# More chunks of the down product in three reduced-precision parts, with the high parts of activations taken by VectorE and ScalarE in turns

## The chip, the cores and the metric

The kernel runs on one core of a Trainium2 chip. The metric is the device time of one execution in microseconds; the kernel before takes 281.24 us (median of three runs, 281.20 to 281.31). One further execution was taken with the profiler, and all durations below come from it.

## What is computed

An attention block with polynomial sketches is followed by a feed-forward block (SwiGLU). Cut to what matters:

```python
# attention: q, k, v are (4, 4, 1088, 32); S1, S2 are (8, 32)
phi(x) = outer(S1 @ x, S2 @ x)             # 64 features per position
kv, z  = sum_s phi(k) v, sum_s phi(k)      # per batch and head
attn   = (phi(q) @ kv) / (phi(q) @ z + 1e-6)
# feed-forward over 4352 tokens of width 128, hidden width 1536
g   = x @ w_gate
out = (g * sigmoid(g) * (x @ w_val)) @ w_out
```

All inputs and outputs are float32.

## The kernel before

Everything is kept transposed: tokens lie along the free dimension, features on partitions. Tokens are cut into blocks: three small ones of batch 0 (384, 384 and 320 tokens), then seven "line" blocks that cover batches 1 to 3, six of 480 tokens and a last one of 384. The line blocks are numbered 0 to 6 here. The hidden width of 1536 is cut into 12 chunks of 128.

The line blocks are worked in one software pipeline over y = 0 to 83 (`END`, the loop at L1355): turn y belongs to block y // 12 and chunk y % 12, which together are one unit. A turn issues, in this order:

- `start_unit(y + 1)`: two matmuls on the "difference" parts of weights and tokens (L977) into a pair of PSUM banks, then ScalarE scales both banks in place (L980).
- `finish_unit(y)`: first the work that earlier turns put down in the table `before` for this turn; then four matmuls that add to the pair (L990, L991); Silu on ScalarE (L993); the gated product on VectorE (L998), which makes the hidden chunk and gives the pair of banks free; then the work that was put down in the table `behind`.
- `down`: the down product of a unit that was finished about five turns earlier.
- `parts_of`: a piece of the attention of batches 2 and 3; in turns 4, 6, 20, 22 and 40 a group of attention matmuls on PE stands ahead of the turn. `token_steps` cut the tokens of the next block into parts in listed turns.

There are three pairs of banks, handed out in turns by `pair`, so the pair of unit y is wanted again by the start of unit y + 3. In turns 20 and 40 (`WIDE`) the finish stands ahead of the next start. The lists fix the order on each engine; there is no planner at run time, and each engine takes its instructions in the order in which they were issued.

The matmuls of gate and value use three products of reduced precision (type fp32r) in place of one of full precision: a number a is cut into a high part a1 = a(1 - 2^-13) rounded to fp32r, a rest a0, and a difference made of both, and the product is put together from difference x difference, high x high and rest x rest. The down product can be done in the same way, and before the change it is for five chunks, (1, 4, 6, 8, 10), of each of blocks 3, 4 and 5 (`FINE`, `DOWN`, L895, L896):

- The parts of the weights are made by `cut_down` (L909), a generator that is taken one step further in each of the turns 24, 26, ... 36 (L1371): ScalarE makes the high part `w1`, GpSimd the rest `low`, ScalarE the scaled rest `wb`, GpSimd the difference `wd`. The other chunks of such a block use weights scaled by -4096 (`scaled`), so that they add to the differences in one bank.
- The parts of a hidden chunk are made by `cut_hidden` (L942): in turn y + 1 ScalarE makes the high part h1 (L954), in turn y + 2 GpSimd the rest h0 (L955), in turn y + 3 VectorE the difference hd (L958). Three sets of buffers serve in turns; they take the place of tiles that the attention no longer needs.
- `down` (L1041) then issues three matmuls (L1054 into one bank, L1056 and L1057 into a second) where it issues one of full precision otherwise (L1062). After chunk 10, `copy_out` has ScalarE copy the second bank (L1077), and after chunk 11 `put_together` has VectorE add the first (L1083); the store follows.

Block 2, and blocks 0, 1 and 6, are done with full-precision down products throughout.

Of the kernel before, what the change touches and what calls it, by code (L numbers as in the profile page):

```python
# [7 lines left out]
FP32 = mybir.dt.float32  # L8
F32R = mybir.dt.float32r
# [3 lines left out]
AF = mybir.ActivationFunctionType  # L13
ALU = mybir.AluOpType
# [5 lines left out]
def kernel(  # L20
# [28 lines left out]
    nc = tc.nc  # L49
    P = nc.NUM_PARTITIONS  # L50
    B, H, S, Dh = q.shape
    R = S1.shape[0]
    D, Dff = moe_w_gate.shape
# [5 lines left out]
    NCH = Dff // P  # L59
# [11 lines left out]
    WB = 480  # L71
# [9 lines left out]
    const = ctx.enter_context(tc.tile_pool(name="const", bufs=1))  # L81
    stage = ctx.enter_context(tc.tile_pool(name="stage", bufs=2))
    apool = ctx.enter_context(tc.tile_pool(name="attn", bufs=1))
# [29 lines left out]
    def bank(tag=None):  # L113

        if tag is not None:
            i = place[tag]
        elif oldest[0]:
            i = min((i for i in used if i not in held), key=used.get)
        else:
            i = place[free_banks[turn[0] % len(free_banks)]]  # L120
            turn[0] += 1
        touch(i)
        return PS[:, i, :]
# [31 lines left out]
    wo = const.tile([P, NCH, D], FP32, name="wo")  # L155
# [32 lines left out]
    def load_next():  # L188
# [36 lines left out]
        out=ident[:], in_=ident[:], pattern=[[-1, P]], base=0, channel_multiplier=1,  # L225
# [90 lines left out]
    late = const.tile([P, NL, BW], FP32, tag="late", name="late", bufs=1)  # L316
# [500 lines left out]
    BETA = 4096.0  # L817
    CUT = 1.0 - 2.0**-13
# [3 lines left out]
    def whole(ap):  # L822
        return ap.bitcast(FP32)
# [17 lines left out]
    def cut_weights(w, lows, engine):  # L841

        rows = [], [], [], []
        sub = dict(op=ALU.subtract)
        for c, (w1, wb, wd) in enumerate(homes(w)):
            src = w[:, 3 * c : 3 * c + 3, :]
            low = lows[c]
            w_parts[id(w), c] = (w1, wb, wd)
            fine = dict(out=wd, in0=whole(w1), in1=whole(wb), **sub), engine.tensor_tensor
            if engine is nc.vector:  # L850
                fine = dict(
                    out=wd, in0=low, scalar=-BETA, in1=whole(w1), op0=ALU.mult, op1=ALU.add
                ), engine.scalar_tensor_tensor
            for row, f, args in zip(
                rows,
                (nc.scalar.activation, engine.tensor_tensor, nc.scalar.activation, fine[1]),
                (
                    dict(out=w1, in_=src, func=AF.Copy, scale=CUT),
                    dict(out=low, in0=src, in1=whole(w1), **sub),
                    dict(out=wb, in_=low, func=AF.Copy, scale=BETA),  # L860
                    fine[0],
                ),
            ):
                row.append((f, args))
        return rows
# [26 lines left out]


    line = list(range(HEAD, len(blocks)))
    FINE, PLAIN = (1, 4, 6, 8, 10), (0, 2, 3, 5, 7, 9, 11)  # L895
    DOWN = [(i, j) for i in line[3:6] for j in FINE]  # L896
    down_parts = {}
    h_parts = {}
    h_sets = []
    before, behind = {}, {}  # L900

    def add_to(where, y, f):
        where.setdefault(y, []).append(f)

    def now(where, y):
        for f in where.pop(y, ()):
            f()

    def cut_down():  # L909

        n = len(FINE)
        parts = const.tile([P, 3, n, D], F32R, tag="late", name="dparts", bufs=1)
        w1, wb, wd = (parts[:, k] for k in range(3))
        scaled = apool.tile([P, len(PLAIN), D], FP32, tag="zs", name="scaled")
        low = [
            apool.tile([P, c, D], FP32, tag=tag, name="low" + tag)[:]
            for tag, c in (("kas", 2), ("kab2", 3))
        ]
        down_parts.update(w1=w1, wb=wb, wd=wd, scaled=scaled)
        cs = slice(0, 2), slice(2, 5)  # L920
        runs = [(0, slice(1, 5, 3)), (2, slice(6, 11, 2))]
        for k, c in runs:
            nc.scalar.activation(w1[:, cs[k > 0]], wo[:, c, :], AF.Copy, scale=CUT)
        yield
        for (k, c), x in zip(runs, low):
            nc.gpsimd.tensor_tensor(
                out=x, in0=wo[:, c, :], in1=whole(w1[:, cs[k > 0]]), op=ALU.subtract
            )
            yield
        for c, x in zip(cs, low):  # L930
            nc.scalar.activation(wb[:, c], x, AF.Copy, scale=BETA)
        yield
        for c in cs:
            nc.gpsimd.tensor_tensor(
                out=wd[:, c], in0=whole(w1[:, c]), in1=whole(wb[:, c]), op=ALU.subtract
            )
            yield
        for k, c in ((0, slice(0, 1)), (1, slice(2, 4)), (3, slice(5, 12, 2))):
            m = len(range(12)[c])
            nc.scalar.activation(scaled[:, k : k + m, :], wo[:, c, :], AF.Copy, scale=-BETA)  # L940

    def cut_hidden(y, i, j):  # L942

        if not h_sets:
            x = []
            for tag in ("kld", "qld", "vld", "kT", "qT"):
                t = const.tile([P, 2, WB], F32R, tag=tag, name="h" + tag, bufs=1)
                x += [t[:, k, :] for k in range(2)]
            h_sets.extend(x[k : k + 3] for k in range(0, 9, 3))
        n = blocks[i][1]  # L950
        h_sets.append(h_sets.pop(0))
        h1, h0, hd = h_parts[i, j] = [x[:, 0:n] for x in h_sets[-1]]
        h = hidden[i, j][:, 0:n]
        add_to(behind, y + 1, lambda: nc.scalar.activation(h1, h, AF.Copy, scale=CUT))  # L954
        add_to(before, y + 2, lambda: nc.gpsimd.tensor_tensor(  # L955
            out=h0, in0=h, in1=whole(h1), op=ALU.subtract
        ))
        add_to(before, y + 3, lambda: nc.vector.scalar_tensor_tensor(  # L958
            out=hd, in0=whole(h0), scalar=-BETA, in1=whole(h1), op0=ALU.mult, op1=ALU.add
        ))  # L960


    room = const.tile([P, 10, BW], FP32, tag="room", name="room", bufs=1)
# [18 lines left out]
    def finish_unit(y):  # L982
        i, j = line[y // NCH], y % NCH
        n = blocks[i][1]
        x1, x0, _ = (x[:, 0:n] for x in x_parts[i])
        ps = sums_of.pop(y)
        now(before, y)
        for k, w in enumerate((wg, wv)):
            w1, wb = (w_parts[id(w), j // 3][t][:, j % 3, :] for t in range(2))
            nc.tensor.matmul(ps[:, k], w1, x1, start=False, stop=False, skip_group_check=True)  # L990
            nc.tensor.matmul(ps[:, k], wb, x0, start=False, stop=True, skip_group_check=True)  # L991
        sg = fpool.tile([P, WB], FP32, tag="sg", name="sg", bufs=5)[:, 0:n]
        nc.scalar.activation(sg, ps[:, 0], AF.Silu, scale=WHOLE)  # L993
        slot_of[i, j] = slots.pop(0)
        hj = slot_of[i, j]
        hidden[i, j] = hj
        todo.append((i, j))
        nc.vector.scalar_tensor_tensor(  # L998
            out=hj[:, 0:n], in0=ps[:, 1], scalar=WHOLE, in1=sg, op0=ALU.mult, op1=ALU.mult
        )  # L1000
        let_go(y)
        now(behind, y)
        if (i, j) in DOWN:
            cut_hidden(y, i, j)
# [36 lines left out]
    def down(y=None):  # L1041
# [3 lines left out]
        if j == 0:  # L1045
            acc[i] = bank("g1" if i == 1 else "g2" if i in line[2::2] else "acc")
        mine = [c for c in range(NCH) if (i, c) in DOWN]
        if mine and j == mine[0]:
# [88 lines left out]
    for h in range(H):  # L1137
# [13 lines left out]
        out=s12[:],  # L1151
        in0=sTv.unsqueeze(1).to_broadcast([P, H, 2, R]),
        in1=own[:].unsqueeze(2).unsqueeze(3).to_broadcast([P, H, 2, R]),
        op=ALU.mult,
# [19 lines left out]
    n = steps[0][1]  # L1174
# [58 lines left out]
    def group():  # L1233
        while ahead[0] != "pe":
            ahead[0] = next(att)
        ahead[0] = next(att, "end")
# [34 lines left out]
    parts = {}  # L1271
# [8 lines left out]
    for z, (i, j) in enumerate(seq):  # L1280
# [16 lines left out]
        if z == 20:  # L1297
# [4 lines left out]
            first, low, second, third = cut_weights(wv, lows, nc.gpsimd)  # L1302
# [48 lines left out]
    oldest[0] = True  # L1351
    hold("acc")
    down_steps = cut_down()
    start_unit(0)
    for y in range(END):  # L1355
        if y in GROUPS:
            group()
        if y in WIDE:
            finish_unit(y)
        if y + 1 < END:  # L1360
            start_unit(y + 1)
        if y not in WIDE:
            finish_unit(y)
        for _ in range(2):

            if len(todo) > min(5 + (todo[0] == (line[1], 0)), END - y + 1):
                down(y)
        parts_of(y < EASY or y % 2 == 0)
        for gen in token_steps.get(y, ()):
            next(gen, None)  # L1370
        if y in range(24, 38, 2):  # L1371
            next(down_steps, None)
    ps = wide("a")[:, 0, 0:D]
    for j in range(NCH):
# [6 lines left out]
    b, x0 = divmod(t0 // 32, NX)  # L1381
# [34 lines left out]
```

## Time and profile before

| | before |
|---|---|
| median of three runs | 281.24 us |
| the profiled execution, whole | 281.56 us |
| its span, first to last instruction | 279.9 us |
| PE (matmul) busy | 273.3 us |
| PEld (weight loads) busy | 195.5 us |
| ScalarE (ACT) busy | 181.5 us |
| VectorE (DVE) busy | 174.3 us |
| GpSimd (POOL) busy | 76.9 us |
| mean granted TensorE clock | 1.000 |
| full-precision matmul records of L1062 on 480 tokens, mean | 565 ns (two records for each matmul) |
| a matmul of parts on 480 tokens, L1054 to L1057, mean | 377 to 382 ns |
| VectorE gated product L998, 480 tokens, mean | 657 ns |
| ScalarE high part L954, mean | 606 ns |
| GpSimd rest L955, mean | 1223 ns |
| VectorE difference L958, mean | 649 ns |

Busy times are the sums of the records' durations. Matmuls are pipelined, so that records overlap and their mean is longer than the spacing of one to the next; the chain of work that ended last shows the spacing. A group's row names the line, engine, operation, output tile and input tiles, shape, count, and then busy time, mean of one, and idle time ahead of it with what ended it. Idle time of an engine that isn't the bound costs nothing by itself.

### The profile page before, as it was taken

The page shows a single profiled execution, that of the slowest core. Times are in us where ns is not written, and L with a number is a line of the kernel's source. Part 1 is how long each engine was busy: PE and PEld are TensorE (multiplying, and loading weights), DVE is VectorE, ACT ScalarE, POOL GpSimd, SP SyncE. Part 2 cuts the span into 40 slices and gives each one's busy share as a digit, 9 for nine tenths or more (in the row PEclk, how much of TensorE's full clock was granted, in tenths as well). Part 3 has the DMA queues.
Part 4 walks back from the last instruction along what each step waited for, and adds up shares of the span by engine and source line. Part 5 has one row for each costly group of instructions (what it writes and reads, how often), then busy time and mean ns, then how long its engine had stood idle before and what let it go on. Part 6 is the DMA issues. An engine that isn't in the chain of part 4 may idle for free.

```text
span 279.9 us, 5561 instructions
## 1 busy us (share of the span) xinstructions
PE 273.3 (98%) x2154; PEld 195.5 (70%) x2154; DVE 174.3 (62%) x327; ACT 181.5 (65%) x323; POOL 76.9 (27%) x93
## 2 busy tenths in 40 slices
PE   7899999999999999999999999999999999999995
PEld 6645565666756687777577767757777778778994
DVE  3997987976688863887544565545436444644431
ACT  3468566555511686677457786869788888877860
POOL 3314422179720530160010140013313333131000
PEclk9999999999999999999999999999999999999999
DMA  6573195222041123000200020002000200100011
GB/s 193 164 226 78 49 284 171 82 80 80 20 108 28 27 85 91 2 1 2 36 13 4 0 39 0 0 2 35 1 0 2 35 0 0 23 15 1 9 30 28
DMA packets 26139, 14.30 MB, mean 51 GB/s; under 512 B 19840, under 2 KB 24192, under 8 KB 26112
## 3 DMA queue, kind: packets, MB, share of 16 engines
q1 hardware_dynamic: 25456, 13.84, 19.2%
q8 instruction: 17, 0.28, 0.4%
q10 hardware_dynamic: 656, 0.10, 0.2%
q14 instruction: 10, 0.08, 0.1%
HBM read 11.41 MB, written 2.23 MB: 49 GB/s over the span
## 4 chain that ended last, share of the span: by engine, by line
PE 94%; DVE 2%; DMA 2%; ACT 1%; issue 0%; SPq 0%
PE PS L1062 26%; PE PS L1014 16%; PE PS L990 13%; PE PS L977 13%; PE PS L991 13%; PE PS L783 2%; PE PS L357 2%; PE PS L345 2%; PE PS L391 2%; DMA kld<-in_k_dram 2%; PE PS L1057 1%; PE PS L1054 1%; PE PS L1056 1%; PE PS L1090 1%; PE PS L500 1%; PE PS L448 1%
## 5 line engine op out<-in xcount | busy, mean ns | idle before, releaser
L980 ACT ACTIVATE PS<-PS 128x960 f32<-128x960 f32 (+1 forms) x84 | 78.3, 934 | 37.1 <-PE PS L977 36.6
L998 DVE SCALAR_TENSOR_TENSOR hbuf<-PS,sg 128x480 f32<-128x480 f32 (+1 forms) x84 | 54.0, 643 | 75.2 <-ACT sg L993 74.9
L1062 PE MATMUL PS<-hbuf,wo 128*128 128x480 f32 (+3 forms) x142 | 57.5, 505 | 0.0
L977 PE MATMUL PS<-xd,gphq 128*128 128x480 f32 (+1 forms) x84 | 52.2, 622 | 0.0
L993 ACT ACTIVATE sg<-PS 128x480 f32<-128x480 f32 (+1 forms) x84 | 46.6, 555 | 2.0 <-PE PS L991 1.3
L990 PE MATMUL PS<-x,graw 128*128 128x480 f32 (+1 forms) x84 | 32.1, 382 | 0.6 <-ACT PS L980 0.6
L1062 PEld LDWEIGHTS PS<-hbuf,wo 128*128 128x128 f32 x142 | 26.6, 189 | 8.2 <-issue 0.9
L991 PE MATMUL PS<-x,wb 128*128 128x480 f32 (+1 forms) x84 | 31.6, 376 | 0.0
L977 PE MATMUL PS<-xd,wd 128*128 128x480 f32 (+1 forms) x84 | 31.4, 374 | 0.0
L990 PE MATMUL PS<-x,w 128*128 128x480 f32 (+1 forms) x84 | 31.4, 374 | 0.0
L991 PE MATMUL PS<-x,graw 128*128 128x480 f32 (+1 forms) x84 | 31.3, 372 | 0.0
L1014 PE MATMUL PS<-xT,wg 128*128 128x384 f32 (+1 forms) x72 | 28.7, 480 | 0.0
L1014 PE MATMUL PS<-xT,wv 128*128 128x384 f32 (+1 forms) x72 | 28.0, 470 | 0.2 <-DVE wv L289 0.2
L1018 ACT ACTIVATE sg<-PS 128x384 f32<-128x384 f32 (+1 forms) x30 | 13.9, 466 | 18.7 <-PE PS L1014 17.0
L977 PEld LDWEIGHTS PS<-xd,gphq 128*128 128x128 f32 x84 | 15.8, 188 | 12.5 <-ACT PS L980 9.6
L977 PEld LDWEIGHTS PS<-xd,wd 128*128 128x128 f32 x84 | 15.9, 189 | 12.2 <-issue 9.0
L1062 PE MATMUL PS<-hbuf,scaled 128*128 128x480 f32 x42 | 20.3, 564 | 0.0
L1014 PEld LDWEIGHTS PS<-xT,wv 128*128 128x128 f32 x72 | 13.4, 190 | 8.9 <-DVE hbuf L1029 0.9
L1014 PEld LDWEIGHTS PS<-xT,wg 128*128 128x128 f32 x72 | 12.9, 189 | 9.3 <-issue 1.2
L883 POOL TENSOR_TENSOR x<-xT,x 128x480 fp32r<-128x480 f32 (+1 forms) x6 | 7.1, 1178 | 42.8 <-ACT x L882 42.8
L990 PEld LDWEIGHTS PS<-x,graw 128*128 128x128 f32 x84 | 15.7, 187 | 4.3 <-ACT PS L980 1.6
L990 PEld LDWEIGHTS PS<-x,w 128*128 128x128 f32 x84 | 15.8, 188 | 2.1
(169 smaller groups left out, 409.8 us busy)
## 6 DMA issues: line engine op xcount, KB each, us to landing
kld<-in_k_dram SPq DMA_DIRECT2D x4, 544.0 KB, 4.4
vld<-in_v_dram SPq DMA_DIRECT2D x12, 144.0 KB, 4.6
qld<-in_q_dram SPq DMA_DIRECT2D x3, 544.0 KB, 3.5
raw<-in_moe_w_out_dram SPq DMA_DIRECT2D x4, 384.0 KB, 4.0
raw<-in_moe_w_gate_dram SPq DMA_DIRECT2D x3, 384.0 KB, 3.7
raw<-in_moe_w_val_dram SPq DMA_DIRECT2D x3, 384.0 KB, 3.6
out_dram<-o SPq DMA_DIRECT2D x16, 60.0 KB, 1.9
vld<-in_v_dram SPq DMA_DIRECT2D x4, 112.0 KB, 4.4
```

Of the source, the lines that this page charges most:

```text
L345: nc.tensor.matmul(ps[32 * a : 32 * a + 32, 96 * (c - c0) : 96 * (c - c0) + 96], qT[:, 4 * c + a, :], s123[:, a : a + H, :, :].rearrange(" ...
L357: nc.tensor.matmul(ps[32 * a : 32 * a + 64, 64 * (c - c0) : 64 * (c - c0) + 64], kT[:, c, a : a + 2, :].rearrange("p a t -> p (a t)"), s12 ...
L883: engine.tensor_tensor(out=x0[:, 0:n], in0=x, in1=whole(x1[:, 0:n]), op=ALU.subtract)
L977: nc.tensor.matmul(ps[:, k], w_parts[id(w), j // 3][2][:, j % 3, :], xd, start=True, stop=True)
L980: nc.scalar.activation(ps, ps, AF.Copy, scale=-1.0 / BETA / WHOLE)
L990: nc.tensor.matmul(ps[:, k], w1, x1, start=False, stop=False, skip_group_check=True)
L991: nc.tensor.matmul(ps[:, k], wb, x0, start=False, stop=True, skip_group_check=True)
L993: nc.scalar.activation(sg, ps[:, 0], AF.Silu, scale=WHOLE)
L998: nc.vector.scalar_tensor_tensor(out=hj[:, 0:n], in0=ps[:, 1], scalar=WHOLE, in1=sg, op0=ALU.mult, op1=ALU.mult)
L1014: nc.tensor.matmul(o[:, 0:n], w[:, j, :], xT[:, t0 : t0 + n], start=True, stop=True)
L1018: nc.scalar.activation(sg[:, 0:n], g[:, 0:n], AF.Silu)
L1062: nc.tensor.matmul(acc[i][:, 0:n], w, hidden[i, j][:, 0:n], **sides)
```

## The change

1. More chunks in parts: in blocks 3 to 5 the chunks 1, 2, 4, 5, 7, 8, 9 and 10 (eight in place of five), and in block 2, which had none, the chunks 2, 4, 6, 8, 9 and 10.
2. The high part of a hidden chunk is made by VectorE for the chunks 2, 5, 8 and 10 of blocks 3 to 5, in the table `before` of turn y + 1; for the others, and all of block 2, by ScalarE as before.
3. The weights' parts are made for ten chunks (1 to 10) and in turns 20 to 28, each step taking pieces of three, three and four chunks; the parts lie in the tile `room`, the rests in the place of the tile `late`.
4. There are six sets of buffers for the parts of hidden chunks; the new ones lie in the place of `late` too, after the rests.

```diff
-    FINE, PLAIN = (1, 4, 6, 8, 10), (0, 2, 3, 5, 7, 9, 11)
-    DOWN = [(i, j) for i in line[3:6] for j in FINE]
+    FINE, PLAIN = range(1, NCH - 1), (0, 1, 3, 5, 7, 6, NCH - 1)
+    DOWN = [(line[2], j) for j in (2, 4, 6, 8, 9, 10)]
+    DOWN += [(i, j) for i in line[3:6] for j in (1, 2, 4, 5, 7, 8, 9, 10)]
...
     def cut_down():
...
-        parts = const.tile([P, 3, n, D], F32R, tag="late", name="dparts", bufs=1)
+        parts = const.tile([P, 3, n, D], F32R, tag="room", name="dparts", bufs=1)
...
+        low = const.tile([P, n, D], FP32, tag="late", name="dlow", bufs=1)
...
+        def high(c):
+            nc.scalar.activation(w1[:, c], wo[:, FINE[0] :][:, c], AF.Copy, scale=CUT)
+        def left(c):
+            nc.gpsimd.tensor_tensor(
+                out=low[:, c], in0=wo[:, FINE[0] :][:, c], in1=whole(w1[:, c]), op=ALU.subtract
+            )
+        def scale(c):
+            nc.scalar.activation(wb[:, c], low[:, c], AF.Copy, scale=BETA)
+        def differ(c):
+            nc.gpsimd.tensor_tensor(
+                out=wd[:, c], in0=whole(w1[:, c]), in1=whole(wb[:, c]), op=ALU.subtract
+            )
+        def other(k, c):
+            m = len(range(NCH)[c])
+            nc.scalar.activation(scaled[:, k : k + m, :], wo[:, c, :], AF.Copy, scale=-BETA)
+        a, b, c = slice(0, 3), slice(3, 6), slice(6, n)
+        for step in (
+            [(high, a)], [(left, a), (high, b)], [(left, b), (scale, a)], [(differ, a), (high, c)],
+            [(left, c), (scale, b)], [(differ, b), (scale, c)], [(differ, c), (other, *rest[0])],
+            [(other, *rest[1])], [(other, *rest[2]), (other, *rest[3])],
+        ):
+            for f, *args in step:
+                f(*args)
             yield
...
     def cut_hidden(y, i, j):
...
-            h_sets.extend(x[k : k + 3] for k in range(0, 9, 3))
+            t = const.tile([P, 8, WB], F32R, tag="late", name="hlate", bufs=1)
+            x += [t[:, k, :] for k in range(8)]
+            h_sets.extend(x[k : k + 3] for k in range(0, 18, 3))
...
-        add_to(behind, y + 1, lambda: nc.scalar.activation(h1, h, AF.Copy, scale=CUT))
+        if j in (2, 5, 8, 10) and i != line[2]:
+            add_to(before, y + 1, lambda: nc.vector.tensor_scalar(h1, h, CUT, None, op0=ALU.mult))
+        else:
+            add_to(behind, y + 1, lambda: nc.scalar.activation(h1, h, AF.Copy, scale=CUT))
...
-        if y in range(24, 38, 2):
+        if y in range(20, 30):
             next(down_steps, None)
```

More of the change, by code (lines that the diff above doesn't have):

```diff
@@ L911, in cut_down @@
         n = len(FINE)
-        parts = const.tile([P, 3, n, D], F32R, tag="late", name="dparts", bufs=1)
+        parts = const.tile([P, 3, n, D], F32R, tag="room", name="dparts", bufs=1)
         w1, wb, wd = (parts[:, k] for k in range(3))
         scaled = apool.tile([P, len(PLAIN), D], FP32, tag="zs", name="scaled")
[L915 to L918, printed above, removed]
+        low = const.tile([P, n, D], FP32, tag="late", name="dlow", bufs=1)
         down_parts.update(w1=w1, wb=wb, wd=wd, scaled=scaled)
[L920 to L925, printed above, removed]
+        rest = [(0, slice(0, 1)), (1, slice(1, 8, 2)), (5, slice(6, 7)), (6, slice(NCH - 1, NCH))]
+        def high(c):
+            nc.scalar.activation(w1[:, c], wo[:, FINE[0] :][:, c], AF.Copy, scale=CUT)
+        def left(c):
             nc.gpsimd.tensor_tensor(
-                out=x, in0=wo[:, c, :], in1=whole(w1[:, cs[k > 0]]), op=ALU.subtract
+                out=low[:, c], in0=wo[:, FINE[0] :][:, c], in1=whole(w1[:, c]), op=ALU.subtract
             )
[L929 to L933, printed above, removed]
+        def scale(c):
+            nc.scalar.activation(wb[:, c], low[:, c], AF.Copy, scale=BETA)
+        def differ(c):
             nc.gpsimd.tensor_tensor(
@@ L936, in cut_down @@
             )
+        def other(k, c):
[9 more added lines that the diff above has]
+                f(*args)
             yield
-        for k, c in ((0, slice(0, 1)), (1, slice(2, 4)), (3, slice(5, 12, 2))):
-            m = len(range(12)[c])
-            nc.scalar.activation(scaled[:, k : k + m, :], wo[:, c, :], AF.Copy, scale=-BETA)
     def cut_hidden(y, i, j):
```

## The prediction

> **What bounds the kernel now.** I read the page first: busy shares, granted clock, the chain that ended last.
>
> ```profile
> PE 273.3 (98%) x2154; PEld 195.5 (70%) x2154; DVE 174.3 (62%) x327; ACT 181.5 (65%) x323; POOL 76.9 (27%) x93
> PEclk9999999999999999999999999999999999999999
> PE 94%; DVE 2%; DMA 2%; ACT 1%; issue 0%; SPq 0%
> ```
>
> PE is the bound: the chain stands on it for 94% of the span, and the clock is at its top digit in all 40 slices. So a matmul that goes away is worth its time, as long as no other engine makes PE wait. Then I asked for the chain between 226 and 234 us, inside the blocks that the change touches (start, length, what).
>
> ```profile
> 226.41 0.43 PE PS L977 x2
> ...
> 227.48 0.22 PE PS L991
> 227.69 0.22 PE PS L1054
> 227.92 0.21 PE PS L1056
> 228.13 0.21 PE PS L1057
> 228.35 0.44 PE PS L977 x2
> ...
> 229.65 0.81 PE PS L1062 x2
> 230.46 0.43 PE PS L977 x2
> ```
>
> One turn of the loop is one unit: two start matmuls (L977), four finish matmuls (L990, L991), one down product. Without parts the down product is one full-precision matmul, 0.81 us (L1062). In parts it is three matmuls, 227.69 to 228.35 = 0.66 us. The turns agree: 226.41 to 228.35 = 1.94 with parts, 228.35 to 230.46 = 2.11 without. No gap stands between matmuls in either. The page's 564 ns for L1062 and 380 ns for a part count overlapping pipelines; the chain's spacing is the price.
>
> Last I read the timelines of the helpers, for how much room they have (start, length, operation, idle before and its releaser). ScalarE in block 2, two turns:
>
> ```profile
> 162.22 0.95 ACT L980 ACTIVATE PS<-PS 128x960 f32<-128x960 f32 x1 [0.69 <-PE PS L977]
> 163.09 0.56 ACT L993 ACTIVATE sg<-PS 128x480 f32<-128x480 f32 x1
> 164.35 0.95 ACT L980 ACTIVATE PS<-PS 128x960 f32<-128x960 f32 x1 [0.69 <-PE PS L977]
> ```
>
> VectorE in the same stretch, and GpSimd's weight differences:
>
> ```profile
> 163.69 0.66 DVE L998 SCALAR_TENSOR_TENSOR hbuf<-PS,sg 128x480 f32<-128x480 f32 x1
> ...
> 166.39 1.33 DVE L380 TENSOR_TENSOR phq<-qab 128x768 f32<-128x768 f32 x1
> ```
>
> ```profile
> L934 POOL TENSOR_TENSOR dparts<-dparts 128x384 fp32r<-128x384 f32 x1 | 1.7, 1724 | 0.0
> L934 POOL TENSOR_TENSOR dparts<-dparts 128x256 fp32r<-128x256 f32 x1 | 0.7, 742 | 4.0 <-ACT dparts L931 4.0
> ```
>
> The reader is to see two rooms and one warning. Back to back, ScalarE's scaling takes 0.87 us before the next instruction starts (162.22 to 163.09), Silu 0.45 (182.17 to 182.62), a high part 0.49 (209.67 to 210.16); so a turn has about 0.7 us of ScalarE idle. The scaling of unit y+1 ends 1.42 us after its two matmuls begin, and they are followed 2.55 us after that beginning by the finish that needs it: ScalarE may be 1.1 us late. VectorE's gating (L998) ends at 164.35, and the unit that takes the same two banks starts at 165.99, two turns after 161.75: 1.6 us of room, 1.3 with short turns. The warning is the L380 at 166.39: 1.33 us where the other eight average 0.95, while GpSimd's L934 pair ran from 166.17; the second L934 took 1.72 us where 1.01 is usual for 384 elements (L926).
>
> **What the Trainium skill says.** "FP8 and Floating Point Precision", TensorE Precision Notes: full FP32 takes four passes through the array, reduced-precision FP32 is one truncated read. The trace agrees: 0.81 against 0.22 us. "SBUF — State Buffer", Who interferes with whom: a VectorE instruction with two SBUF inputs, or one in a two-port mode, and a GpSimd instruction that reads SBUF exclude each other, and the later one waits for the whole of the other. The 1.33 and 1.72 above agree.
>
> **The change part by part.**
> (1) Chunks in parts: 3 x 5 = 15 become 3 x 8 + 6 = 30. Each of the 15 new ones saves 0.81 - 0.66 = 0.15 us by its product, 0.17 by the turns shown; over 205.91 to 234.52 the turns average 1.955 and 2.11, so I take 0.155. 15 x 0.155 = 2.3 us off PE. Bounds 15 x 0.15 = 2.25 and 15 x 0.17 = 2.55. PE gets no other instruction; scaled weights for the other chunks of block 2 are full-precision products as before.
> (2) High parts. 12 of the 30 go to VectorE, so ScalarE has 18 where it had 15. In block 2 all six are ScalarE's: 0.87 + 0.45 + 0.49 = 1.81 us in a turn of 1.955, so it fits. For blocks 3 to 5, twelve turns take PE 8 x 1.955 + 4 x 2.11 = 24.1 us, ScalarE 12 x 1.32 + 4 x 0.49 + about 1 (sum copy, token part) = 18.8. Nothing on PE.
> (3) VectorE's high part, a scalar multiply of 480 elements, is not in the trace. Nearest rows: the scalar operation of L267, 352 ns for 384 elements, and L998's 657 ns, which would be the value without a faster mode. "VectorE: DVE Perf Modes", the perf-mode tier table, gives this operation two elements per cycle on fp32 in SBUF; the 96 further elements are 96 / 2 / 0.96 = 50 ns, so I take 0.40 us, range 0.36 to 0.66. With it come 15 more low-to-difference steps (L958, 0.65 us). Per block: 12 x 0.58 (start to start) + 8 x 0.65 + 4 x 0.40 + some 2 = 15.8 of 24.1 us.
> (4) GpSimd: 15 more low parts of 1.22 us. Per block 8 x 1.22 + 1.21 = 11 of 24.1 us.
> (5) The weights' parts are cut for ten chunks in turns 20 to 28, where they were cut for five in turns 24 to 36. ScalarE: 0.53 + 0.53 + 0.63 for the high parts, the same for the scaled lows = 3.4 us against 1.9; other chunks 1.6 against 1.4. GpSimd about 6.6 us against 4.2. Mostly one piece per turn of at most 0.57 us start to start, inside ScalarE's 0.7 us. The exception is turn 27: the four-chunk scaling, the first high part and block 3's token part, 0.53 + 0.49 + 0.49 = 1.5, overshoots by 0.7 to 0.8, inside the 1.1; turn 28 adds two of 0.26 to 0.31, turn 29 a high part, and the overshoot shrinks each time. In turns 20 and 22 the attention's copies are served by PE groups of 1.6 to 3.4 us, which give ScalarE more room still. No DMA is issued, and the queue of SP is passed by nothing new; block 2's store comes one turn later.
> (6) Block 2 gets a sum copy (ScalarE, 0.58) and a putting together (VectorE, 0.65). The copy lands in turn 40, behind that turn's Silu and ahead of the scaling at 188.69, which PE already waits for by about 0.04 us at 189.70. Silu starts at 187.82, so the copy runs 188.27 to 188.76: the scaling is 0.07 late, and PE with it. I put 0.1.
> (7) New buffers. The low weights and more activation sets take the place of the tile that held batch 3's key features, whose last reader is PE in turn 20 (139.17 to 140.4); the first write is in turn 21. Six sets in place of three: the closest reuse is eight turns later, the product five. Bank "acc" is read for block 1 in turn 28, written by block 2's parts about turn 31. No wait I can find.
> (8) Queueing on VectorE. The difference step stands ahead of the gating in its queue. For chunks 7 to 10 in a row, the low part of the next chunk starts on GpSimd just ahead of the difference step, so this waits up to 1.22 us, runs 0.62, a high part 0.40 follows: gating starts about 0.8 us late, within 1.3. The pair of ports is held 1.22 + 0.65 + half of 0.40 = 2.07 us per turn of 1.955: 0.1 per turn behind, 0.4 over four turns, then plain turns repay it. A token step in the same turn could use up the room; I put 0.1 us for a few such moments, between 0 and 1.5.
>
> Sum: -2.33 + 0.1 + 0.1 = -2.1. Against the profiled execution, 279.9 in the span and 1.66 around it = 281.56: 279.4. The median shown is 0.32 below that execution, so 281.24 - 2.1 = 279.1.
>
> **The rivals.**
> A, the forecast, 0.76: the helpers stay inside their room; 279.1, own range 278.7 to 279.6.
> B, partial stalls, 0.13: ScalarE in block 2 or blocked difference steps exceed the room now and then. For it: ScalarE's full durations add to 0.95 + 0.56 + 0.60 = 2.11, not under 1.955; and turns with parts never stood side by side before. Against: the turns at 209.98 had high part, token part and scaling back to back, and PE kept 1.96. If half of the gain goes: 281.24 - 1.1 = 280.1.
> C, no change, 0.04: three parts in a row are no shorter, because weight loads show. Nine loads at 0.19 = 1.7 of 1.955 us. Against: six in a row already pass at 0.217 each. 281.2. That the change does not do what it says falls here too; the emitted PE order shows 30 chunks with three products.
> D, slower, 0.07: the shared ports. If every low part takes the blocked 1.72 us and the high part 0.66, a turn needs 1.72 + 0.65 + 0.33 = 2.70, 0.75 behind per turn; four turns make 3.0, less 1.3 of room = 1.7 of PE waiting for banks per block, 5.1 over three blocks, which gives 281.24 - 2.3 + 5.1 = 284.0. It decides from 0.5 us behind per turn on (4 x 0.5 - 1.3 = 0.7, three times 2.1). Against: all fifteen low parts of before average 1.22 and all fifteen differences 0.65, with 2.8 us and more of GpSimd idle ahead of most.
>
> **How the numbers follow.** Less than 0.2% (0.56 us) can't be told from no change here. A and B are faster: 0.89; C the same: 0.04; D slower: 0.07. The range takes A and most of B, 278.7 to 280.5; the likeliest stays 279.1.
>
> **What would show it.** the full-precision down product falls from 105 instructions (210 records, two each) to 90 (180), with 30 of each part; turns with parts stay at 1.95 to 1.97 even for chunks 7 to 10; ScalarE's idle ahead of the scaling shrinks but PE's idle stays under 0.5 us; VectorE's high part takes about 0.4 us. Wrong would be PE idle with ScalarE's scaling or VectorE's gating as releaser, difference steps of 1.5 us and more, or a granted clock below the top digit.

## The result, and the profile after

The changed kernel takes 279.42 us (median of four runs, 279.39 to 279.52) where the kernel before takes 281.27 (281.20 to 281.31): ratio 0.9935, 95% interval 0.9918 to 0.9952. It is 1.85 us faster; forecast were 2.1 us and 279.1, in a range from 278.7 to 280.5.

The page of the changed kernel: busy shares, granted clock, and the share of the chain by engine.

```profile
PE 270.8 (98%) x2169; PEld 197.8 (71%) x2169; DVE 204.0 (73%) x355; ACT 184.6 (66%) x330; POOL 98.8 (36%) x110
PEclk9999999999999999999999999999999999999999
PE 94%; DVE 2%; DMA 1%; ACT 1%; issue 0%; SPq 0%
```

PE still carries 94% of the chain at the top digit of its clock. VectorE's busy time rose by 30 us and GpSimd's by 22, nearly all of it beside PE. What PE itself waited for, in the table of waits of the changed kernel (instruction, releaser, total us, times, longest):

```profile
PE PS L357 <- DVE kT L330: 0.9, 1, 0.9
PE PS L1003 <- ACT PS L993: 0.6, 1, 0.6
```

These are the longest but for the program's first instruction, and they are old: the kernel before has 0.7 and 0.6 in the same places, at the start of the program and in turn 0 of the loop. Next, the chain through two neighbouring turns with parts (start, length, what); the lines moved by the diff, so L990 is the start, L1003 and L1004 the finish, L1067 to L1070 the down product.

```profile
204.62 0.44 PE PS L990 x2
...
205.93 0.22 PE PS L1067
206.15 0.22 PE PS L1069
206.37 0.23 PE PS L1070
206.60 0.43 PE PS L990 x2
...
208.34 0.21 PE PS L1070
208.56 0.44 PE PS L990 x2
```

204.62 to 206.60 is 1.98 and 206.60 to 208.56 is 1.96: chunks 8 and 9 of block 3, side by side, at about the pace that a lone one had before.

Whole profiles of two kernels can't be compared to a tenth here, since the first load of keys landed 4.41 us after its issue in the profile of before and 4.08 in the one after, and everything behind it starts earlier by that much. So I compare stretches between the same points, from the start matmuls of one turn to those of the next. From turn 23 on:

| turns | before | after | gain | 0.155 times the new chunks |
|---|---|---|---|---|
| 23 to 28 (weights' parts are cut) | 12.75 | 12.75 | 0 | 0 |
| 29 to 38 (chunks 2 to 9 of block 2) | 21.19 | 20.36 | 0.83 | 0.78 |
| 39 (chunk 10 of block 2, then the attention's group) | 5.23 | 5.23 | 0 | 0.16 |
| 40 and 41 | 3.47 | 3.56 | -0.09 | 0 |
| 42 to 70 | 59.22 | 58.26 | 0.96 | 1.24 |
| 71 to 76 (shorter matmuls) | 10.86 | 10.69 | 0.17 | 0.16 |
| sum | | | 1.87 | 2.33 |

The sum agrees with the 1.85 of the medians. Two things are missing from the full 2.33: turns 39 to 41, and 0.28 in turns 42 to 70.

Part of the 0.28 is the price itself. Counted from first finish matmul to first finish matmul over turns 42 to 69, the 12 turns with parts of the kernel before average 1.956 us and the 16 without 2.104, a difference of 0.149 and not 0.155. In the changed kernel 19 turns with parts average 1.960 and 9 without 2.116. So about 0.05 of the 0.28 is the price, and about 0.2 is that turns of both kinds became a little longer.

Turn 39 shows how a saved matmul can be worth nothing. The chain of before there, and then that of the changed kernel:

```profile
184.03 0.22 PE PS L991
184.25 0.81 PE PS L1062 x2
185.05 2.02 PE PS L783 x39
187.07 0.43 PE PS L990
```

```profile
182.92 0.23 PE PS L1004
183.15 0.01 issue
183.17 0.58 ACT sg L1006
183.75 0.02 issue
183.77 0.67 DVE hbuf L1011
184.44 0.04 issue
184.48 1.49 PE PS L783 x35
185.97 0.43 PE PS L1003
```

Before, PE looks busy throughout, and the chain stays on it. After, the chain leaves PE: the attention's matmuls (L783) need the banks that the gated product of turn 39 gives free. From the last finish matmul of turn 39 to the first of turn 40 it is 187.07 - 184.03 = 3.04 and 185.97 - 182.92 = 3.05 us. The timeline of weight loads of before had said the same:

```profile
184.98 0.15 PEld L783 LDWEIGHTS PS<-phT,spread 32*32 32x32 f32 x6 [0.70 <-ACT sg L993]
185.59 1.00 PEld L783 LDWEIGHTS PS<-phT,spread 32*32 32x32 f32 x58 [0.46 <-DVE hbuf L998]
```

Six weight loads of the group went at 184.98, and the other 58 weight loads waited until 185.59, just after the gated product ended at 184.88 + 0.66 = 185.54. The wait was there before, with the full-precision product standing in front of it.

The helpers' rows of the changed kernel, VectorE's high parts (L965) and differences (L971), and a stretch of its timeline:

```profile
L971 DVE SCALAR_TENSOR_TENSOR hlate<-hlate 128x480 fp32r<-128x480 f32 x10 | 11.0, 1100 | 0.0
L965 DVE TENSOR_SCALAR hlate<-hbuf 128x480 fp32r<-128x480 f32 x4 | 2.5, 625 | 0.1
```

```profile
211.45 1.03 DVE L887 SCALAR_TENSOR_TENSOR xd<-x,x 128x480 fp32r<-128x480 f32 x1
212.40 1.68 DVE L971 SCALAR_TENSOR_TENSOR hqT<-hkT 128x480 fp32r<-128x480 f32 x1
214.00 0.64 DVE L1011 SCALAR_TENSOR_TENSOR hbuf<-PS,sg 128x480 f32<-128x480 f32 x1
```

A difference that took 0.65 us before averages 1.10 in this row and 1.01 over all 30. The high part takes 0.36 to 0.41 us in seven of its twelve records (the forecast had 0.40), and up to 1.34 beside GpSimd. In this stretch the gated product starts at 214.00, 1.57 us after its Silu ended at 212.43; normally it is 0.03. PE did not wait for it, so 1.57 was just inside the room.

### The profile page after: what moved, and what is told of

It is laid out like the page before. It is cut to its first block, busy times and chain, and to the rows that moved or that the text cites. A ratio compares the mean times of both kernels' runs of the same rounds, so it can differ in the third digit from the quotient of the medians.

```text
span 277.7 us, 5659 instructions
## 1 busy us (share of the span) xinstructions
PE 270.8 (98%) x2169; PEld 197.8 (71%) x2169; DVE 204.0 (73%) x355; ACT 184.6 (66%) x330; POOL 98.8 (36%) x110
## 4 chain that ended last, share of the span: by engine, by line
PE 94%; DVE 2%; DMA 1%; ACT 1%; issue 0%; SPq 0%
PE PS L1075 22%; PE PS L1027 16%; PE PS L1003 13%; PE PS L990 13%; PE PS L1004 13%; PE PS L1067 2%; PE PS L1070 2%; PE PS L1069 2%; PE PS L357 2%; PE PS L783 2%; PE PS L345 2%; PE PS L391 2%; DMA kld<-in_k_dram 1%; PE PS L1103 1%; PE PS L500 1%; PE PS L448 1%
## 5 line engine op out<-in xcount | busy, mean ns | idle before, releaser
L990 PE MATMUL PS<-xd,gphq 128*128 128x480 f32 (+1 forms) x84 | 47.1, 561 | 0.0
L1075 PE MATMUL PS<-hbuf,wo 128*128 128x480 f32 (+3 forms) x118 | 45.9, 492 | 0.0
L1003 PE MATMUL PS<-x,graw 128*128 128x480 f32 (+1 forms) x84 | 32.1, 382 | 0.6 <-ACT PS L993 0.6
L1004 PE MATMUL PS<-x,wb 128*128 128x480 f32 (+1 forms) x84 | 31.6, 376 | 0.0
L990 PE MATMUL PS<-xd,wd 128*128 128x480 f32 (+1 forms) x84 | 31.4, 374 | 0.0
L1003 PE MATMUL PS<-x,w 128*128 128x480 f32 (+1 forms) x84 | 31.4, 374 | 0.0
L1004 PE MATMUL PS<-x,graw 128*128 128x480 f32 (+1 forms) x84 | 31.3, 373 | 0.0
L1075 PEld LDWEIGHTS PS<-hbuf,wo 128*128 128x128 f32 x118 | 22.1, 189 | 7.4 <-issue 0.9
L990 PEld LDWEIGHTS PS<-xd,gphq 128*128 128x128 f32 x84 | 15.8, 188 | 9.9 <-ACT PS L993 6.4
L990 PEld LDWEIGHTS PS<-xd,wd 128*128 128x128 f32 x84 | 15.8, 189 | 9.7 <-issue 6.2
L1003 PEld LDWEIGHTS PS<-x,graw 128*128 128x128 f32 x84 | 15.7, 187 | 4.4 <-ACT PS L993 1.6
L1075 PE MATMUL PS<-hbuf,scaled 128*128 128x480 f32 x36 | 17.4, 565 | 0.0
L1003 PEld LDWEIGHTS PS<-x,w 128*128 128x128 f32 x84 | 15.8, 188 | 2.2
```

What stands on the lines that cost most here:

```text
L990: nc.tensor.matmul(ps[:, k], w_parts[id(w), j // 3][2][:, j % 3, :], xd, start=True, stop=True)
L1075: nc.tensor.matmul(acc[i][:, 0:n], w, hidden[i, j][:, 0:n], **sides)
```

## The experiments

Each kernel is the changed one with the edit shown. Medians of one kernel differ by some tenths between sets of runs (the kernel before took 281.27 to 281.62 in the five sets), so beside the median stands the time between the first finish matmuls of turns 23 and 83 in the kernel's one trace, "the turns": before 121.84, changed 119.96 (119.95 when it was traced again in another set of runs). Single turns are counted here from first finish matmul to first finish matmul, unless "start to start" is said. A wait of PE between the start and the finish matmuls then counts to a turn one lower than in the table above and in the expectations.

**Without block 2.**

```diff
-    DOWN = [(line[2], j) for j in (2, 4, 6, 8, 9, 10)]
+    DOWN = []
```

> The changed kernel without parts in block 2; blocks 3 to 5 keep eight chunks each. Room theory (PE is the bound, the helpers fit; the shortfall sits in turns 39 to 41 and in runs of turns with parts): block 2 brings 0.83 us in turns 29 to 38, nothing in turn 39, and costs 0.09 in turn 41, so this takes 0.74 us longer than 279.42: 280.15. Rival, ScalarE has no room in block 2, where it makes every high part: the six chunks bring little, 279.4 to 279.7. The forecast's own price, 6 x 0.155 - 0.1 = 0.83, gives 280.25.

Measured 280.29 us beside 281.44 for the kernel before; the turns 120.72, that is 0.76 more than the changed kernel. Block 2's six chunks bring what the table says, 0.83 - 0.09. ScalarE has room there.

**Chunk 7 for chunk 10 in block 2.** The scaled weights of chunk 10 take the place of those of 7.

```diff
-    DOWN = [(line[2], j) for j in (2, 4, 6, 8, 9, 10)]
+    DOWN = [(line[2], j) for j in (2, 4, 6, 7, 8, 9)]
```

> In block 2 chunk 7 is done in parts in place of chunk 10, so that turn 39, whose group of attention matmuls waits for VectorE's gated product, has a full-precision product in front of it again, and the sum copy comes one turn earlier, away from the scaling that turn 41 waits for. Room theory: the 0.155 us of turn 39 and the 0.09 of turn 41 come back, 279.42 - 0.24 = 279.18, with turn 39 at about 5.23 us from start to start and the turn of chunk 7 at 1.96. Rival, the shortfall is not there but spread over all turns: 279.4.

Measured 279.28 us beside 281.44; the turns 119.73, 0.23 less, as the room theory has it. Turn 36, where chunk 7 is used, fell from 2.12 to 1.96; from start to start, turn 39 has a full product again and still takes 5.23, and turn 41 is back at 2.24 from 2.32. The median lies between the two forecasts, so it is the turns that decide. So the chunk in turn 39 was worth nothing and the sum copy in front of the scaling cost 0.08.

**All high parts on ScalarE.**

```diff
-        if j in (2, 5, 8, 10) and i != line[2]:
+        if False:
```

> All high parts on ScalarE, no turns with VectorE. Room theory: ScalarE needs 0.87 + 0.45 + 0.49 = 1.81 us in a turn of 1.96, and 18.8 + 4 x 0.49 = 20.8 us of 23.9 in a block, so PE does not wait and the time stays at 279.4, within 0.15. Rival, ScalarE becomes the bound without VectorE's share: the four turns in a row plus token part and sum copy overshoot the 1.1 us of room, PE waits for the scaling, and 0.5 us or more are lost per block, 280.9 or more.

Measured 279.51 us beside 281.44; the turns 119.95, and no turn differs from the changed kernel's by more than 0.02. PE does not wait: VectorE's share of the high parts is not needed at eight chunks.

**Ten chunks in blocks 3 to 5.**

```diff
-    DOWN += [(i, j) for i in line[3:6] for j in (1, 2, 4, 5, 7, 8, 9, 10)]
+    DOWN += [(i, j) for i in line[3:6] for j in FINE]
```

> Ten chunks (1 to 10) in parts in blocks 3 to 5 in place of eight. Room theory: six more chunks at 0.12 to 0.155 us, 279.42 - 0.7 to 0.9 = 278.5 to 278.7. Rival, the ports that VectorE and GpSimd share become the bound: 1.22 + 0.65 + 0.16 = 2.03 us or more are held in each of ten turns of 1.955, with blocked steps of 1.3 to 1.7 us; the gated product falls behind by more than 1.3 us, PE waits for banks, and the time is 279.4 or more.

Measured 281.17 us beside 281.44; the turns 121.59, 1.63 more than with eight chunks. The rival's number came true. The trace shows where, against the changed kernel: turn 40 grew by 0.49, turn 43 by 0.3, turn 44 by 1.36, turn 54 by 0.25, and all other turns with parts stay at 1.95 to 1.98, ten in a row too. VectorE's timeline, then GpSimd's, in turns 42 to 44:

```profile
192.44 1.65 DVE L971 SCALAR_TENSOR_TENSOR hqT<-hkT 128x480 fp32r<-128x480 f32 x1 [0.47 <-POOL hkT L968]
194.01 0.67 DVE L1117 STREAM_TRANSPOSE o<-sum 128x480 f32<-128x480 f32 x1
194.60 0.36 DVE L965 TENSOR_SCALAR hlate<-hbuf 128x480 fp32r<-128x480 f32 x1
194.89 0.64 DVE L1011 SCALAR_TENSOR_TENSOR hbuf<-PS,sg 128x480 f32<-128x480 f32 x1
195.46 1.39 DVE L887 SCALAR_TENSOR_TENSOR xd<-x,x 128x480 fp32r<-128x480 f32 x1
196.77 1.67 DVE L971 SCALAR_TENSOR_TENSOR hlate<-hlate,hqT 128x480 fp32r<-128x480 f32 x1
198.36 0.65 DVE L1011 SCALAR_TENSOR_TENSOR hbuf<-PS,sg 128x480 f32<-128x480 f32 x1
```

```profile
192.35 1.22 POOL L968 TENSOR_TENSOR hlate<-hbuf,hqT 128x480 fp32r<-128x480 f32 x1
195.11 2.81 POOL L968 TENSOR_TENSOR hlate<-hbuf,hlate 128x480 fp32r<-128x480 f32 x2 [1.54 <-DVE hlate L965]
```

The difference at 192.44 began just after GpSimd's low part at 192.35 and ended about 0.5 us after that did (193.57); the next two steps with two inputs in SBUF took 1.39 and 1.67 beside GpSimd's pair at 195.11. Two gated products came late, and PE stood:

```profile
199.06 0.48 PE L990 MATMUL PS<-xd,wd 128*128 128x480 f32 x1 [1.25 <-DVE hbuf L1011]
```

What remained open was whether the ports bound any long run, or only this meeting of store, token part and blocked steps.

**Ten chunks in blocks 4 and 5 only.** With the edit of block 2 from above.

```diff
-    DOWN += [(i, j) for i in line[3:6] for j in (1, 2, 4, 5, 7, 8, 9, 10)]
+    DOWN += [(i, j) for i in line[3:6] for j in ((1, 2, 4, 5, 7, 8, 9, 10) if i == line[3] else FINE)]
```

> Chunk 7 for chunk 10 in block 2, eight chunks in block 3, ten in blocks 4 and 5. Pile-up theory (the loss of the ten-chunk kernel lies in turns 40 to 45, where block 2's sum copy, putting together and store, the next block's token part and block 3's first parts meet; in a steady run even ten turns in a row fit, ports and all): 0.24 us less by the chunk moved, 4 x 0.14 = 0.56 less by the four new chunks, up to 0.3 back in turn 54, where block 3's sum is put together: 278.6 to 278.9. Rival, the shared ports of VectorE and GpSimd bound every long run: no better than 279.2.

Measured 278.95 us beside 281.62; the turns 119.38, 0.58 less than the changed kernel. The median is 0.05 above the range of the pile-up theory and 0.25 below the rival's number. The ports do not bound a long run: turns 55 to 63 stay at 1.94 to 1.98. Turn 54, where block 3's sum is put together, gives back 0.27: behind two blocked differences (1.68 and 1.10 us) VectorE's putting together ended at 216.33, and the first product of block 4's parts into the bank that it had read came at 216.38.

**Ten chunks, token part later.** Ten chunks in blocks 3 to 5, the edit of block 2, and:

```diff
-        for at in {1: (3, 8), 2: (20, 21), 3: (27, 32), 4: (40, 42)}.get(m, (NCH * m - 10, NCH * m - 9)):
+        for at in {1: (3, 8), 2: (20, 21), 3: (27, 32), 4: (44, 45)}.get(m, (NCH * m - 10, NCH * m - 9)):
```

> Ten chunks in blocks 3 to 5, chunk 7 for chunk 10 in block 2, and block 4's token part moved from turns 40 and 42 to turns 44 and 45, three turns away from block 2's sum. Pile-up theory: the 1.7 us of waiting for VectorE's gated product in turn 45 goes or falls under 0.5 us, and the time is 278.3 to 278.9. Rival, the ports: with ten blocked steps in a row the wait stays wherever the token part stands, 280.5 or more.

Measured 279.58 us beside 281.62; the turns 120.11. Neither number: the waits of turns 43 and 44 went, and turn 46 became 0.93 longer (2.88). What PE waits for there is not the gated product but the moved token part itself:

```profile
201.39 0.46 PE L990 MATMUL PS<-xd,gphq 128*128 128x480 f32 x1 [0.68 <-DVE xd L887]
```

The first start of block 4, at the head of turn 47, needs `xd`, the difference of the block's tokens, and turn 45 is a late place for it. VectorE began it at 200.13, behind a high part that took 1.44 us beside GpSimd, and it took 1.11 itself. So the edit brought in a deadline that the other kernels do not have. The run speaks against the rival, since ten chunks in a row make no wait in turns 43 and 44 with the token part elsewhere and the sum one turn earlier. It does not show whether a token part without the store is enough for the pile-up.

**Ten chunks without GpSimd.** Ten chunks in blocks 3 to 5, block 2 and the token part as in the change, all high parts on ScalarE, and the low parts of blocks 3 to 5 on VectorE:

```diff
-        add_to(before, y + 2, lambda: nc.gpsimd.tensor_tensor(
+        low_engine = nc.gpsimd if i == line[2] else nc.vector
+        add_to(before, y + 2, lambda: low_engine.tensor_tensor(
```

> Ten chunks in blocks 3 to 5 with the token part where the change has it, but in these blocks ScalarE makes every high part and VectorE, not GpSimd, every low part: no step of GpSimd runs beside the parts of a run of turns except the token part. VectorE's own work rises from 1.4 to 0.58 + 0.65 + 0.65 = 1.88 us per turn of 1.955, and its differences should all take 0.65 us. If the blocking of the ports is what made the ten-chunk kernel wait in turn 45, that wait shrinks and the time is 279.0 to 279.6 with the ScalarE wait of turn 41 left; if it is VectorE's sheer load in those turns, the wait grows and the time is 281.2 or more.

Measured 279.10 us beside 281.62; the turns 119.56. The waits of turns 43, 44 and 54 are gone (1.96, 1.96, 1.97), though VectorE has more steps; only the 0.49 in turn 40 is left, where ScalarE has a high part and the sum copy ahead of the scaling. The groups of this kernel, differences (L972 here) and low parts on VectorE (L969):

```profile
L972 DVE SCALAR_TENSOR_TENSOR hqT<-hkT 128x480 fp32r<-128x480 f32 x6 | 3.9, 647 | 0.0
L969 DVE TENSOR_TENSOR hlate<-hbuf,hlate 128x480 fp32r<-128x480 f32 x10 | 6.5, 651 | 0.0
```

With ten chunks and GpSimd the first of these rows had 1312 ns, and VectorE was busy for 207.7 us in all, against 204.0 here. The edit also took the high parts off VectorE; with eight chunks that alone changed nothing (the third experiment), with ten it was not tried alone. So it was GpSimd's steps beside VectorE's that cost the time, not the amount of work on VectorE.

**Five chunks in every second turn, and five in a row.** These ask for the 0.28 us missing in turns 42 to 70. No parts in block 2; the table of scaled weights is fitted to the chunks left over.

```diff
-    DOWN = [(line[2], j) for j in (2, 4, 6, 8, 9, 10)]
-    DOWN += [(i, j) for i in line[3:6] for j in (1, 2, 4, 5, 7, 8, 9, 10)]
+    DOWN = []
+    DOWN += [(i, j) for i in line[3:6] for j in (2, 4, 6, 8, 10)]   # the second: (4, 5, 6, 7, 8)
```

> No parts in block 2, five chunks (2, 4, 6, 8, 10) of blocks 3 to 5 in parts, every second turn. It is the set of before with one chunk moved, so 281.2 to 281.4. If turns with parts are worth more alone than side by side (0.18 against 0.14 us, from the turns of before and after), this is 0.4 to 0.5 us faster than the five side by side; if not, equal within 0.1.

> No parts in block 2, five chunks (4 to 8) of blocks 3 to 5 in parts, side by side. If turns with parts are worth more alone than side by side, 281.7, 0.4 to 0.5 us slower than the five in every second turn; if not, 281.2 to 281.4 like them.

Measured 281.80 and 281.58 us beside 281.43, both above the 281.2 to 281.4 of the forecasts; the turns 121.99 and 121.95. Neither by the turns nor by the medians is every second turn the faster, so the idea that neighbours are worth less falls. The two also show that blocked steps by themselves need not cost time: VectorE's 15 differences average 0.65 us in the first and 1.27 in the second. But both stand 0.15 and 0.11 above before's 121.84, with as many chunks in parts, and the difference of the first lies in turns 45 to 71 (55.02 us, 54.86 before). This points to some 0.1 of the 0.28 as the cost of the new arrangement (six sets, other places of the parts) and not of the number of chunks. Which of its pieces costs it was not tried, and where the rest is stays open.

**A better version.** The changed kernel was run again beside two versions on one chip. Both have ten chunks in blocks 3 to 5, low parts of these on VectorE, and high parts on ScalarE but for one, so that the scaling of turn 41 is not held up; the second has seven chunks in block 2.

```diff
-        if j in (2, 5, 8, 10) and i != line[2]:
+        if (i, j) == (line[3], 3):
...
-    DOWN = [(line[2], j) for j in (2, 4, 6, 8, 9, 10)]
+    DOWN = [(line[2], j) for j in (2, 4, 6, 7, 8, 9)]   # the second: (2, 4, 5, 6, 7, 8, 9)
```

> The changed kernel as it is, beside the next two on the same chip: 279.4 if the chip is like the first, up to 279.7 on one where the kernel before takes 281.6.

> Ten chunks in blocks 3 to 5 with low parts on VectorE and high parts on ScalarE (VectorE takes that of chunk 3 in block 3, so that ScalarE is free for the scaling in turn 41), and chunk 7 for chunk 10 in block 2. No wait is left in turns 40 to 45, 46 and 54: against the changed kernel 0.24 less by block 2 and 6 x 0.14 = 0.84 less by the new chunks, 1.0 us faster in all, give or take 0.2. If VectorE's 1.88 us per turn leave no room after all, 0.4 or less.

> As the one with everything mended, and chunk 5 of block 2 in parts too: 0.14 us faster again if ScalarE keeps its room in turns 27 to 31, where weights, tokens and high parts meet; else slower by the wait for the scaling in turns 29 to 31.

Measured 279.44 (changed again), 278.91 and 279.73 us, beside 281.53 for the kernel before; ratios to before 0.9913 (0.9881 to 0.9945), 0.9903 (0.9871 to 0.9934) and 0.993 (0.9908 to 0.9952). The intervals overlap; the turns tell them apart: 119.95, 119.13 and 120.09. The first version is 0.82 us shorter there, inside the 1.0 give or take 0.2. By the medians it is only 0.53, outside that range; in its trace the first load of keys landed 0.33 us later than in that of the changed kernel (4.46 and 4.13 us). It is the fastest by the turns of all kernels run.

Turn 44 still loses 0.26. VectorE made a low part in 1.67 us beside GpSimd's token step (at 189.47) and has no gap in its row from there on, though GpSimd does nothing more until 200. The gated product at 196.15 starts 1.55 us after its Silu ended. So here VectorE's own work leaves it no time to catch up after one blocked step.

The second version fails, and not where I looked: PE waits in turn 34 (2.94 us in place of 2.11), and not for ScalarE. In its table of waits, and in VectorE's timeline:

```profile
PE PS L991 <- DVE hbuf L1012: 0.7, 1, 0.7
```

```profile
172.78 1.68 DVE L972 SCALAR_TENSOR_TENSOR hlate<-hlate,hqT 128x480 fp32r<-128x480 f32 x1
174.38 0.65 DVE L1012 SCALAR_TENSOR_TENSOR hbuf<-PS,sg 128x480 f32<-128x480 f32 x1
```

That is VectorE's gated product again. It starts 2.25 us after its Silu ended (172.13): ahead of it stand a transpose of the attention (0.96 us), block 3's token part (0.61) and this difference, which began just after a low part of GpSimd (172.69). In block 2 the low parts are still GpSimd's.

## Why the prediction was right, point by point

**The bound and the price of a chunk, (1).** Right in kind: PE stays the bound, the records of full-precision down products fell from 210 to 180 as forecast, the turns with parts hold 1.94 to 1.99 side by side, and taking block 2 away costs 0.76. The step that was mis-sized is "15 x 0.155 = 2.3": 14 chunks had a price, since the one in turn 39 stood in front of a wait that was already there (0 in place of 0.155; moving it got 0.16 back, as the second experiment shows), and turns 42 to 70 gave 0.96 for a net eight chunks, 0.12 each. The price came from averages over one stretch; over turns 42 to 69 of the same trace it would have been 0.149, which is 0.05 of the 0.28 that is missing there. The new arrangement seems to cost another 0.1 at an equal number of chunks, and the last 0.1 is not settled. Nothing was checked for the turns with an attention group, where the weight loads' timeline showed the wait.

**ScalarE, (2) and (5).** Right. The cut of the weights cost nothing in turns 23 to 28 (12.75 both times), the overshoot in turns 27 to 29 reached no matmul, and all high parts on ScalarE give the same turns (119.95 against 119.96). Rival B found no place there.

**VectorE's high part, (3), and GpSimd, (4).** 0.36 to 0.41 us alone, where 0.40 was taken. That the bound of 0.66 would hold for a slower mode was too narrow: beside GpSimd it took up to 1.34.

**The sum copy, (6).** 0.1 forecast, 0.09 measured, in the turn and by the mechanism named.

**Queueing on VectorE, (8).** The mechanism was right and its size too small: not 0.8 but up to 1.57 us late, since token part and difference were both blocked; the 0.1 us put down for it was 0, because the room held. That was partly luck: the product that started at 214.00 ended at 214.64, and the start that takes its banks came at 214.76, after two turns without parts. The room of 1.3 that the prediction gave for short turns would have been too small. The prediction's sign of being wrong, difference steps of 1.5 us and more, came five times (1.68 to 1.70) without making PE wait.

The Trainium skill, "SBUF — State Buffer", Who interferes with whom, says that a VectorE instruction with two SBUF inputs, or one in a two-port mode, and a GpSimd instruction that reads SBUF exclude each other, and that the later one waits for the whole of the other. The runs agree. In the changed kernel 14 of the 30 differences began while a low part ran on GpSimd, and each ended 0.51 to 0.52 us after that low part did; the other 16 took 0.61 to 0.65. With GpSimd's low parts moved away in blocks 3 to 5, 35 of 36 take 0.61 to 0.65.

**Rival D.** Its place and kind were right, as ten chunks show (1.63 us longer than eight) and ten without GpSimd show (the waits gone); its arithmetic of falling behind in every turn was wrong, since ten turns in a row run at 1.94 to 1.98 and PE waits for VectorE only where a token part, a store or a putting together meets blocked steps.

**The sum.** -2.33 + 0.155 + 0.09 + 0.28 - 0.06 (block 2 and turns 71 to 76 gave a little more) = -1.87 in place of -2.1.

## What to carry to other kernels

Price a saved matmul by the turn in which it stands: where the next group on PE already waits for another engine, the saving only lengthens that wait, and the timeline of weight loads shows it before any chain does. Before work is spread over VectorE and GpSimd, look for steps with two SBUF inputs on both sides: putting such work on one of them alone can be faster though that engine then does more. Room is used up where rare steps meet (a sum, a store, the next block's parts), so check those turns one by one and not by averages.

## What the runs showed of the hardware that I had not expected

- A VectorE step that met a running low part of GpSimd ended a fixed time after it, in the changed kernel's trace: the 14 differences 0.51 to 0.52 us after, the five scalar multiplies of 128 x 480 float32 0.27 us after. So a multiply of 0.36 to 0.41 us took 1.33 to 1.34 where GpSimd had begun 0.15 or 0.16 us before it.
- The product of chunks whose parts lay in the last of the six sets took turns of 1.98 to 1.99 us where others took 1.94 to 1.97 (turns 49, 58 and 67, in the changed kernel and with all high parts on ScalarE alike). With ten chunks in each block and GpSimd's low parts moved away, the same set took 1.96 to 1.98 like the others, so the place alone does not explain it. The cause was not tried.
